# Moving the weight transfers of the third and fourth expert: two into the last quarter of attention, the rest between the late gathers

## The chip, the cores and the metric

The kernel runs on 1 core of one Trainium2 chip. The metric is the device time of one execution in microseconds (us), the median of three runs. The engines are TensorE (PE; its weight loads are listed as PEld), VectorE (DVE), ScalarE (ACT), GpSimd (POOL) and SyncE (SP). POOL and SP also issue DMA transfers.

## The reference

Causal attention over 4 batches, 8 heads, 768 positions and head size 64. Three heads attend to everything before them, five only to 4 sink positions and a window of 64. The result, as 3072 tokens of 512 features, goes through a mixture of experts: each token is sent to the one of 8 experts that its domain number names.

```python
def _attn_ref(q, k, v, is_retrieval, n_sink, window):
    scores = scale * np.matmul(q, k.transpose(0, 1, 3, 2))
    ...
    mask = np.where(retr[0, :, 0, 0, None, None], full_mask, stream_mask)
    scores = np.where(mask[None, :, :, :], scores, -1000000000.0)
    ...
    return np.matmul(a, v).astype(np.float32)

def _moe_ref(x, domain_id, w1, w2):
    for e in range(E):
        mask = domain_id == e
        h = np.maximum(x[mask] @ w1[e], 0.0)
        out[mask] = h @ w2[e]
```

## The kernel before, in words

**Attention.** Two heads of one batch make a pair; there are 16 pairs, n = 0 to 15. In iteration n the kernel first calls `hooks(n)` (line 751), then computes the scores of pair n and, between them on PE, the transposes of pair n+1 (`t_items`) and the product with v of pair n-1 (`av_items`). `hooks(n)` asks SP for the loads of pair n+4, POOL for the casts to fp16 of q and k of pair n+2 and of v of pair n+1, and then for the weight transfers listed in `ws` (line 764). When a batch is done, `store_x` writes its tokens to the internal DRAM tensor `x_tok` through SP. `hooks(14)` also gathers the first four token groups of experts 0 and 1.

**Experts.** Experts are taken in pairs `pr`. Seven gathers of 128 rows (`load_xe(pr, g)`, indirect DMAs issued by POOL) bring the tokens of a pair from `x_tok`; group 6 holds the last 64 rows of each of the two experts. `x_transpose(pr, g)` turns them on PE, `layer1(e, c0, c1)` multiplies by w1 and applies the relu, `layer2(e)` multiplies by w2, copies each 128x512 block from PSUM into an `oute` buffer on DVE (four such buffers) and scatters it to the output by an indirect DMA issued by POOL (`finish_group`). `layer2_half(pr)` does group 6 of both experts.

**Weights.** `load_w(e, which)` brings w1 or w2 of expert e (numbered from 0), 2 MB of fp32 in DRAM, as 1 MB of fp16. POOL issues it, because it converts. There are four w1 buffers and four w2 buffers, so w1 of expert 4 waits until expert 0 has used its own.

**What sets the order.** The schedule is manual: on each engine, instructions run in the order in which the program writes them. POOL runs the casts, the weight transfers, the gathers and the scatters in that one order, and all of its transfers go into the one DMA queue q0; the loads and stores of SP go into q1. After attention the order for POOL is: three gathers of pair 0 (lines 799 and 800), seven gathers of pair 1 (line 803), then w2 of expert 1, w1 and w2 of expert 2, w1 and w2 of expert 3 (lines 805 to 808), w1 of experts 4 and 5 (line 813), seven gathers of pair 2 (line 824), w1 of expert 6 (line 827), and only then the three scatters of expert 0.

Of the kernel before, what the change touches and what calls it, by code (L numbers as in the profile page):

```python
# [21 lines left out]
def kernel(  # L22
# [117 lines left out]
    def load_qk(n):  # L140
        b, pi = divmod(n, 4)
        hA, hB = PAIRS[pi]
        for nm, src in (("q", q), ("k", k)):
            t = qkpool.tile([P, 2, NSO, D], FP32, tag=nm, name=f"{nm}32_{n}")
            nc.sync.dma_start(
                out=t[:].rearrange("p h t d -> p h (t d)"),
                in_=hsel(src, b, hA, hB).rearrange("h (p t) d -> p h (t d)", p=P),
            )
            q32_t[nm, n] = t

    def cast_qk(n, engs=None):
        for x, nm in enumerate("qk"):
            t = tpool.tile([P, NSO, 2, D], FP16, tag=f"{nm}16", name=f"{nm}_{n}")
            eng = engs[x] if engs else nc.gpsimd
            eng.tensor_copy(  # L155
                out=t[:].rearrange("p t h d -> p h t d"), in_=q32_t[nm, n][:]
            )
            qk_t[nm, n] = t

    def load_v(b, pi):  # L160
        hA, hB = PAIRS[pi]
        t = vpool.tile([P, 2, NSO, D], FP32, tag="v32", name=f"v32_{b}_{pi}")
        for hh, h in enumerate((hA, hB)):
            nc.sync.dma_start(
                out=t[:, hh], in_=v[b, h].rearrange("(c p) d -> p c d", p=P)
            )
        v_t[b, pi] = t

    def cast_v(b, pi):
        if pi == 0:  # L170
            ve_t[b] = vepool.tile([P, NSO, H, D + 1], FP16, tag="ve", name=f"ve_{b}")
            vs_t[b] = vepool.tile([36, H, D + 1], FP16, tag="vs", name=f"vs_{b}")
            nc.gpsimd.memset(ve_t[b][:, :, :, D : D + 1], 1.0)
        hA, hB = PAIRS[pi]
        for hh, h in enumerate((hA, hB)):
            nc.gpsimd.tensor_copy(out=ve_t[b][:, :, h, 0:D], in_=v_t[b, pi][:, hh])  # L176

    def load_w(e, which):
        if which == 1:
            t = wpool.tile([P, 2, 2, F], FP16, tag="w1", name=f"w1_{e}")  # L180
            nc.gpsimd.dma_start(
                out=t[:].rearrange("p c r f -> p c (r f)"),
                in_=moe_w1[e].rearrange("(c p r) f -> p c (r f)", p=P, r=2),
            )
        else:
            t = wpool.tile([P, 2, 4, DM], FP16, tag="w2", name=f"w2_{e}")
            nc.gpsimd.dma_start(
                out=t[:].rearrange("p c r d -> p c (r d)"),
                in_=moe_w2[e].rearrange("(c p r) d -> p c (r d)", p=P, r=4),
            )  # L190
        w_t[e, which] = t
# [75 lines left out]
    def t_items(n):  # L267

        items = []
        for nm, store in (("q", qT), ("k", kT)):  # L270
            cell = {}

            def tr(t, nm=nm, store=store, cell=cell):
                if t == 0:
                    cell["ps"] = ps_t.tile([P, NSO, P], FP16, tag="tp", name=f"tp{nm}_{n}")
                nc.tensor.transpose(  # L276
                    out=cell["ps"][:, t, :], in_=qk_t[nm, n][:, t].rearrange("p h d -> p (h d)"), identity=id_sb
                )
                if t == NSO - 1:
                    d = tpool.tile([P, P, NSO], FP16, tag=f"{nm}T", name=f"{nm}T_{n}")  # L280
                    nc.vector.tensor_copy(  # L281
                        out=d[:], in_=cell["ps"][:].rearrange("d t p -> d p t")
                    )
                    store[n] = d[:].rearrange("d p t -> d (p t)")
                    ra, rb = (retr[h] for h in PAIRS[n % 4])
                    if nm == "k" and not ra and not rb:
                        ks = ks_t[n % 2]
                        nc.vector.tensor_copy(out=ks[0:64, 0:4], in_=store[n][0:64, 0:4])
                        nc.vector.tensor_copy(
                            out=ks[64:128, 32:36], in_=store[n][64:128, 0:4]  # L290
                        )

            for t in range(NSO):
                items.append((60, lambda t=t, tr=tr: tr(t)))
        return items
# [114 lines left out]
    def store_x(b):  # L410
        nc.sync.dma_start(
            out=x_d[1 + b * S : 1 + (b + 1) * S, :].rearrange("(t p) d -> p t d", p=P), in_=xb[b][:]
        )
# [211 lines left out]
    NG = PAIRSLOTS // P  # L625

    def load_xe(pr, g, nb=B):
        if pr not in xe_t:
            xe_t[pr] = vepool.tile([P, NG, DM], FP16, tag="ve", name=f"xe_{pr}")
        s = pr * NG + g  # L630
        nc.gpsimd.indirect_dma_start(  # L631
            out=xe_t[pr][:, g, :],
            out_offset=None,
            in_=x_d[0 : 1 + nb * S, :],
            in_offset=bass.IndirectOffsetOnAxis(ap=map_i[:, s : s + 1], axis=0),
            bounds_check=nb * S,
            oob_is_err=False,
        )
# [23 lines left out]
    def layer1(e, c0, c1):  # L662
        if e not in hT_t:
            hT_t[e] = epool.tile([P, 8, CAP], FP16, tag="eT", name=f"hT_{e}")
        for f2 in range(4):
            ps = ps_s.tile([P, 1024], FP32, tag="sp", name=f"h1_{e}_{f2}_{c0}")
            pv = ps[:].rearrange("p (a c) -> p a c", a=2)
            for a in range(2):
                fc, fr = divmod(2 * f2 + a, 4)
                for c in range(4):  # L670
                    nc.tensor.matmul(  # L671
                        out=pv[:, a, c0:c1],
                        lhsT=w_t[e, 1][:, c // 2, c % 2, fc * 512 + fr : (fc + 1) * 512 : 4],
                        rhs=xT_t[e][:, c, c0:c1],
                        start=(c == 0),
                        stop=(c == 3),
                    )
            nc.scalar.activation(  # L678
                out=hT_t[e][:, 2 * f2 : 2 * f2 + 2, c0:c1], in_=pv[:, :, c0:c1], func=AF.Relu
            )  # L680
# [30 lines left out]
    def layer2_half(pr):  # L711
        ps = ps_a.tile([P, 512], FP32, tag="av", name=f"o2h_{pr}")
        for f in range(8):
            for i in range(2):
                e = 2 * pr + i
                nc.tensor.matmul(
                    out=ps[i * HALF : (i + 1) * HALF, :],
                    lhsT=hT_t[e][:, f, MAIN:CAP],
                    rhs=w_t[e, 2][:, f // 4, f % 4, :],
                    start=(f == 0),  # L720
                    stop=(f == 7),
                    skip_group_check=True,
                )
        finish_group(pr, 6, ps)
# [23 lines left out]
    def vs_copy(b):  # L748
        nc.vector.tensor_copy(out=vs_t[b][32:36], in_=ve_t[b][0:4, 0])

    def hooks(n):
        b, pi = divmod(n, 4)
        if n + 4 < NPAIR:
            load_qk(n + 4)
            load_v((n + 4) // 4, (n + 4) % 4)
        if n + 2 < NPAIR:
            cast_qk(n + 2)
        if n + 1 < NPAIR:
            cast_v((n + 1) // 4, (n + 1) % 4)
        if pi == 3:  # L760
            vs_copy(b)
        if n >= 5 and n % 4 == 1:
            store_x(n // 4 - 1)
        ws = {4: (0, 1), 8: (1, 1), 12: (0, 2)}
        if n in ws:
            load_w(*ws[n])
        if n == 14:
            for g in (0, 1, 3, 4):
                load_xe(0, g, 3)

    for _, fn in t_items(0):
        fn()
# [27 lines left out]
        load_xe(0, g)  # L800
    for e in range(N_EARLY):
        layer1(e, 0, EARLY)
    for g in range(NG):
        load_xe(1, g)
    load_w(1, 2)
    for e in (2, 3):
        load_w(e, 1)
        load_w(e, 2)
    for g in (2, 6, 5):
        x_transpose(0, g)  # L810
    for e in range(N_EARLY):
        layer1(e, EARLY, CAP)
        load_w(e + 4, 1)
    for e in range(E):
        pr, i = divmod(e, 2)
        nxt = e + 2
        if i == 1:
            layer2_half(pr)
        if nxt < E:
            if i == 0:  # L820
                for g in range(7):
                    x_transpose(pr + 1, g)
                if pr + 2 < E // 2:
                    [load_xe(pr + 2, g) for g in range(NG)]
            layer1(nxt, 0, CAP)
            if nxt + 4 < E:
                load_w(nxt + 4, 1)
        layer2(e)
        if e + 4 < E:
            load_w(e + 4, 2)  # L830
# [96 lines left out]
```

## Time and profile before

| | us |
|---|---|
| median of 3 runs | 257.03 |
| lowest and highest of them | 255.66, 266.19 |
| the profiled execution, device time | 254.73 |
| its span, first to last instruction | 253.0 |
| PE busy in it | 202.8 (80%) |
| POOL busy | 110.2 (44%) |
| DVE busy | 105.5 (42%) |
| ACT busy | 92.6 (37%) |

All positions in the text are microseconds from the start of that span. Busy shares are averages over stages with different limits; a busy PE is not PE at its peak.

### The profile page before, as it was taken

To read this page: it belongs to the slowest core of one execution; us is meant where nothing else is said; L and a number is where in the kernel's file an instruction comes from. 1 tells how busy PE (TensorE), PEld (TensorE's weight loads), DVE (VectorE), ACT (ScalarE), POOL (GpSimd) and SP (SyncE) were. 2 spreads that over 40 slices of the span, in tenths; PEclk is the share of its full clock that TensorE was granted. 3 is DMA by queue.
4 is the path that set the end of the run, shared out by engine and by line. 5 is a ranking of instruction groups with operands and counts; after the bars stand their busy time and mean duration, and the time that the engine had idled before them with its cause. 6 is when DMAs were issued, how large, how long until landed. Compare 5 with 4: busy or idle time off the path is not lost. (4 is left out here: it accounts for less than half of the span.)

```text
span 253.0 us, 4605 instructions
## 1 busy us (share of the span) xinstructions
PE 202.8 (80%) x1871; PEld 120.8 (48%) x1871; DVE 105.5 (42%) x242; ACT 92.6 (37%) x109; POOL 110.2 (44%) x143
## 2 busy tenths in 40 slices
PE   1589899988999999869604999507899979999960
PEld 0246556655666666869401545203545445454420
DVE  1259999997578576501400031004222150403330
ACT  2277547744875876253200504100222305050000
POOL 0557564562455523067932122364757140414550
PEclk9999959997999999997955899956999999999995
DMA  6999999999999842233599999899995856212421
GB/s 218 299 311 305 285 294 254 329 322 244 293 325 226 153 142 72 78 109 97 109 214 216 211 216 216 209 227 237 271 265 174 167 155 135 92 36 84 156 86 37
DMA packets 45467, 49.77 MB, mean 197 GB/s; under 512 B 27263, under 2 KB 38784, under 8 KB 45442
## 3 DMA queue, kind: packets, MB, share of 16 engines
q0 software_dynamic: 7936, 26.75, 45.9%
q1 hardware_dynamic: 36928, 22.02, 31.6%
q10 hardware_dynamic: 578, 0.66, 0.9%
q8 instruction: 16, 0.26, 0.4%
q14 instruction: 9, 0.07, 0.1%
HBM read 56.76 MB, written 10.49 MB: 266 GB/s over the span
## 5 line engine op out<-in xcount | busy, mean ns | idle before, releaser
L332 ACT ACTIVATE eT<-sp 128x1024 f16<-128x1024 f32 (+2 forms) x68 | 60.5, 916 | 35.4 <-PE sp L311 34.8
L678 ACT ACTIVATE hT<-h 128x896 f16<-128x896 f32 (+2 forms) x40 | 30.7, 768 | 96.1 <-PE h L671 96.1
L671 PE MATMUL h<-xT,w 128*128 128x448 f16 (+2 forms) x320 | 54.0, 331 | 11.6 <-DMA w<-in_moe_w_dram 10.8
L684 DVE COPY oute<-o 128x512 f32<-128x512 f32 x24 | 16.6, 692 | 88.5 <-PE o L702 70.1
L702 PE MATMUL o<-w,hT 128*128 128x512 f16 x192 | 44.4, 389 | 10.0 <-DVE oute L684 10.0
L631 POOL DMA_INDIRECT xe<-x_tok,map_i x28 | 28.4, 1013 | 47.9 <-DMA w<-in_moe_w_dram 23.8
L671 PEld LDWEIGHTS <-w 128*128 128x128 f16 x320 | 35.2, 117 | 29.3 <-DMA w<-in_moe_w_dram 11.0
L686 POOL DMA_INDIRECT out_dram<-oute,out_i x28 | 27.9, 997 | 42.4 <-DVE oute L684 37.1
L702 PEld LDWEIGHTS <-hT 128*128 128x128 f16 x192 | 19.0, 99 | 33.6 <-issue 12.4
L386 PE MATMUL av<-ve,eT 128*128 128x65 f16 (+3 forms) x532 | 31.8, 198 | 3.2 <-DVE xb L399 3.2
L386 PEld LDWEIGHTS <-eT 128*128 128x128 f16 (+3 forms) x572 | 25.9, 101 | 13.8 <-issue 4.1
L311 PE MATMUL sp<-qT,kT 64*128 64x192 f16 (+6 forms) x244 | 26.7, 282 | 1.8 <-DVE kT L281 1.2
L311 PE MATMUL sp<-c16s 128*128 128x128 f16 (+1 forms) x132 | 25.9, 279 | 0.4 <-ACT eT L332 0.3
L155 POOL CAST q<-q 128x768 f16<-128x768 f32 x15 | 12.9, 862 | 30.6 <-PE tpq L276 14.5
L281 DVE COPY qT<-tpq 128x768 f16<-128x768 f16 x16 | 15.3, 954 | 7.6 <-PE tpq L276 7.5
L399 DVE TENSOR_TENSOR xb<-av,rcp 128x384 f16<-128x384 f32 x32 | 17.8, 557 | 1.1
L155 POOL CAST k<-k 128x768 f16<-128x768 f32 x16 | 13.5, 842 | 9.9 <-DMA k<-in_k_dram 8.0
L311 PEld LDWEIGHTS <-kT 64*128 64x128 f16 x244 | 9.7, 95 | 16.1 <-issue 7.0
L281 DVE COPY kT<-tpk 128x768 f16<-128x768 f16 x16 | 15.2, 948 | 3.6 <-PE tpk L276 3.6
L176 POOL CAST ve<-v 128x384 f16<-128x384 f32 x32 | 16.0, 528 | 0.7 <-DMA v<-in_v_dram 0.7
L654 DVE COPY xT<-xtp 128x512 f16<-128x512 f16 x24 | 9.1, 418 | 15.2 <-PE xtp L647 14.2
L647 PE MATMUL xtp<-c16s,xe 128*128 128x128 f16 x112 | 10.3, 226 | 6.2 <-DVE xT L654 3.1
(71 smaller groups left out, 123.6 us busy)
## 6 DMA issues: line engine op xcount, KB each, us to landing
w<-in_moe_w_dram POOLq DMA_DIRECT2D x16, 1024.0 KB, 11.3
q<-in_q_dram SPq DMA_DIRECT2D x16, 384.0 KB, 6.0
k<-in_k_dram SPq DMA_DIRECT2D x16, 384.0 KB, 6.0
v<-in_v_dram SPq DMA_DIRECT2D x32, 192.0 KB, 5.7
x_tok<-xb SPq DMA_DIRECT2D x4, 768.0 KB, 6.0
xe<-x_tok,map_i POOLq DMA_INDIRECT x28, 4.8
out_dram<-oute,out_i POOLq DMA_INDIRECT x28, 2.8
c16s<-c ACTq DMA_DIRECT2D x1, 336.5 KB, 4.6
```

What stands on the lines that cost most here:

```text
L155: eng.tensor_copy(out=t[:].rearrange("p t h d -> p h t d"), in_=q32_t[nm, n][:])
L281: nc.vector.tensor_copy(out=d[:], in_=cell["ps"][:].rearrange("d t p -> d p t"))
L311: nc.tensor.matmul(out=sp[:, c : c + w], lhsT=lhsT, rhs=rhs, start=bank not in begun, stop=True, skip_group_check=True,)
L332: nc.scalar.activation(out=eT[n][:, r, c0:c1], in_=sp[:, c0:c1], func=AF.Exp, scale=scale)
L386: nc.tensor.matmul(out=ps[m0:m1, it, :], lhsT=eT[n][kk, r, c : c + w], rhs=rhs, start=(x == 0), stop=(x == len(mms) - 1), skip_group_check ...
L399: nc.vector.tensor_tensor(out=xb[b][:, :, h * D : (h + 1) * D], in0=ps[:, :, 0:D], in1=rcp[:].unsqueeze(2).to_broadcast([P, NSO, D]), op=A ...
L631: nc.gpsimd.indirect_dma_start(out=xe_t[pr][:, g, :], out_offset=None, in_=x_d[0 : 1 + nb * S, :], in_offset=bass.IndirectOffsetOnAxis(ap= ...
L671: nc.tensor.matmul(out=pv[:, a, c0:c1], lhsT=w_t[e, 1][:, c // 2, c % 2, fc * 512 + fr : (fc + 1) * 512 : 4], rhs=xT_t[e][:, c, c0:c1], st ...
L678: nc.scalar.activation(out=hT_t[e][:, 2 * f2 : 2 * f2 + 2, c0:c1], in_=pv[:, :, c0:c1], func=AF.Relu)
L684: nc.vector.tensor_copy(out=o[:], in_=ps[:])
L686: inst = nc.gpsimd.indirect_dma_start(out=out, out_offset=bass.IndirectOffsetOnAxis(ap=out_i[:, s : s + 1], axis=0), in_=o[:], in_offset=None,
L702: nc.tensor.matmul(out=ps[:], lhsT=hT_t[e][:, f, g * P : (g + 1) * P], rhs=w_t[e, 2][:, f // 4, f % 4, :], start=(f == 0), stop=(f == 7),)
```

## The change

Six weight transfers are issued at other places in POOL's order; nothing is added or removed. w2 of expert 0 goes from `hooks(12)` to `hooks(11)`; w1 of expert 2 takes its place in `hooks(12)`; w2 of expert 1 follows the four gathers in `hooks(14)`. After attention, w1 of expert 3 is issued ahead of the gathers of pair 1, w2 of expert 2 between the fourth and the fifth of these gathers, and w2 of expert 3 after w1 of expert 4.

```diff
-        ws = {4: (0, 1), 8: (1, 1), 12: (0, 2)}
+        ws = {4: (0, 1), 8: (1, 1), 11: (0, 2), 12: (2, 1)}
         if n in ws:
             load_w(*ws[n])
         if n == 14:
             for g in (0, 1, 3, 4):
                 load_xe(0, g, 3)
+            load_w(1, 2)
...
     for e in range(N_EARLY):
         layer1(e, 0, EARLY)
-    for g in range(NG):
+    load_w(3, 1)
+    for g in range(4):
         load_xe(1, g)
-    load_w(1, 2)
-    for e in (2, 3):
-        load_w(e, 1)
-        load_w(e, 2)
+    load_w(2, 2)
+    for g in range(4, NG):
+        load_xe(1, g)
     for g in (2, 6, 5):
         x_transpose(0, g)
     for e in range(N_EARLY):
         layer1(e, EARLY, CAP)
         load_w(e + 4, 1)
+        if e == 0:
+            load_w(3, 2)
```

## Rows read from the trace of the kernel before

**Rows 1.** PE in order of time, second half: start, length, operation, [idle before <-releaser]

```profile
121.59 0.61 PE L647 MATMUL xtp<-c16s,xe 128*128 128x128 f16 x8
...
136.36 8.62 PE L671 MATMUL h<-xT,w 128*128 128x448 f16 x32 [10.78 <-DMA w<-in_moe_w_dram]
...
158.02 3.62 PE L702 MATMUL o<-w,hT 128*128 128x512 f16 x16
171.67 3.57 PE L702 MATMUL o<-w,hT 128*128 128x512 f16 x8 [10.04 <-DVE oute L684]
175.04 0.77 PE L647 MATMUL xtp<-c16s,xe 128*128 128x128 f16 x8
...
178.93 6.24 PE L671 MATMUL h<-xT,w 128*128 128x448 f16 x32 [0.39 <-DVE xT L657]
```

**Rows 2.** The waits by engine: who waited for what, us, times, longest

```profile
DVE oute L684 <- DMA out_dram<-oute,out_i: 18.5, 2, 18.2
```

**Rows 3.** POOL in order of time, from the end of attention

```profile
109.08 1.00 POOL L631 DMA_INDIRECT xe<-x_tok,map_i  x1 [11.32 <-SPq L833]
...
121.82 0.78 POOL L187 DMA_DIRECT2D w<-in_moe_w_dram  x1
...
125.36 1.53 POOL L181 DMA_DIRECT2D w<-in_moe_w_dram  x2
127.19 1.08 POOL L631 DMA_INDIRECT xe<-x_tok,map_i  x1 [0.30 <-issue]
132.26 1.04 POOL L631 DMA_INDIRECT xe<-x_tok,map_i  x1 [3.99 <-DMA w<-in_moe_w_dram]
...
161.31 0.75 POOL L181 DMA_DIRECT2D w<-in_moe_w_dram  x1 [4.16 <-DMA w<-in_moe_w_dram]
```

**Rows 4.** Issues with KB, us to landing: at 126.05, 127.19, 156.16, 161.31, 205.53

```profile
w<-in_moe_w_dram POOLq DMA_DIRECT2D x1, 1024.0 KB, 34.7
xe<-x_tok,map_i POOLq DMA_INDIRECT x1, 34.0
xe<-x_tok,map_i POOLq DMA_INDIRECT x1, 7.2
w<-in_moe_w_dram POOLq DMA_DIRECT2D x1, 1024.0 KB, 8.8
w<-in_moe_w_dram POOLq DMA_DIRECT2D x1, 1024.0 KB, 7.9
```

**Rows 5.** Stretches: length, engines' busy us (instructions), PEclk, DMA share, GB/s

```profile
112.00:122.00 10.00, 8.48 (x84) 7.78 (x85) 1.34 (x4) 3.74 (x9) 7.87 (x9) 0.83 0.36 105
126.00:136.00 10.00, 0.00 (x0) 0.00 (x0) 0.10 (x1) 0.00 (x0) 3.01 (x4) 0.58 1.05 209
144.80:161.60 16.80, 16.80 (x89) 8.30 (x88) 2.77 (x4) 4.58 (x5) 3.29 (x4) 1.00 1.05 235
```

**Rows 6.** POOL in order of time, last quarter of attention

```profile
77.68 0.83 POOL L155 CAST q<-q 128x768 f16<-128x768 f32 x1 [1.89 <-PE tpq L276]
...
80.15 0.71 POOL L187 DMA_DIRECT2D w<-in_moe_w_dram  x1
...
92.70 1.09 POOL L631 DMA_INDIRECT xe<-x_tok,map_i  x1 [7.00 <-DVE xb L399]
```

**Rows 7.** DMA queues by packets, MB, share: 58 to 64, then 77 to 82

```profile
q0 software_dynamic: 227, 0.93, 78.3%
q1 hardware_dynamic: 492, 0.54, 29.2%
...
q1 hardware_dynamic: 2049, 1.05, 80.7%
```

**Rows 8.** Issue view: SP's last v load, issued at 76.16

```profile
v<-in_v_dram SPq DMA_DIRECT2D x1, 192.0 KB, 5.7
```

**Rows 9.** PE in order of time, end of attention

```profile
92.76 0.51 PE L276 MATMUL tpq<-c16s,q 128*128 128x128 f16 x6
...
101.82 0.72 PE L647 MATMUL xtp<-c16s,xe 128*128 128x128 f16 x8 [0.65 <-DVE xT L654]
```

## The prediction

> **What bounds the kernel now.** I read the timeline of PE first, because PE is the busiest engine (80% of the span) and the question is where it stands still. After attention two gaps carry nearly all of it [rows 1]: 10.78 us before the first layer of expert 2 at 136.36, ended by a weight transfer, and 10.04 us in the middle of layer 2 of expert 1 at 171.67, ended by a copy into an output buffer on DVE. From 175.04 to the end PE runs with small gaps only.
>
> I then ask what each gap waits for at its source. The first is a transfer by its name: w1 of expert 2, second of seven weight transfers that POOL issues in a row between 121.82 and 126.05 [rows 3]. The second is POOL's order: DVE waited 18.2 us for a scatter to read its buffer out [rows 2], and the scatters stand in POOL's queue behind seven gathers of pair 2 and w1 of expert 6. The gather at 127.19 goes out at once, the next at 132.26 only when a weight has landed, and w1 of expert 6 at 161.31 likewise [rows 3]. Counting places from the first of the seven weights, the gather at 132.26 is the ninth: each issue waits here for the one eight places ahead to land. So POOL is held until the last of the seven, issued at 126.05 and 34.7 us under way, lands at 160.8 [rows 4].
>
> Two prices come out of the same rows. Seven gathers and one weight released one by one between 132.26 and 161.31 make 29.05 / 6 = 4.8 to 4.9 us for each weight in a chain. That the queue is served in order shows in the gather issued at 127.19, which lands 34.0 us later at 161.2, just behind the last weight; the last of that gather group lands at 156.16 + 7.2 = 163.4 [rows 4], so a gather queued in this way costs (163.4 - 161.2) / 6 = 0.37 us. A weight alone takes 7.9 to 8.8 us [rows 4]. The stretch from 126 to 136 shows the DMA engines full (share 1.05) with PE at zero [rows 5]: in that stage the kernel is bound by q0.
>
> **Step 1: two weights in late attention.** w2 of expert 0 is now issued when the casts of `hooks(11)` are done, at 77.68 - 1.89 = 75.8, and w1 of expert 2 in the old slot at 80.15 [rows 6]. For POOL this is free: an issue takes 0.7 to 0.8 us and the slot at 75.8 has 1.89 us of idle time. What it meets is SP's loads. From 77 to 82 q1 still moves 1.05 MB, and the last v load lands at 76.16 + 5.7 = 81.9 [rows 7, 8]. While a weight ran beside SP's loads, from 58 to 64, q1 got 0.54 MB in 6 us, 90 GB/s [rows 7]. At that rate 1.05 MB take 11.7 us and land at 88.7, 7 us later than now. Cover: pair 15 is transposed on PE at 92.76 [rows 9], 4 us later, and its q and k, which SP loads ahead of v, can be cast before the last v load lands. So nothing reaches PE. The store of batch 2 shares its time with the second weight; I let the first gather slip 1.9 us from 92.70 [rows 6]. PE takes the last two of these four groups at 101.82 [rows 9], after idling for a copy and not for a gather: price 0, with an upper bound of 2 us, the whole slip, if that cover is gone.
>
> The Trainium skill ("DMA: Bandwidth & Descriptors", sections "Queues, rings and completion order" and "Issuing engines are not separate DMA queues") speaks against this step: all issuing engines share the same 16 DMA engines, and these take turns between queues packet by packet. The trace shows the sharing but not even turns: 227 packets of q0 beside 492 of q1 [rows 7]. With strict turns q1 would move 227 packets of its mean 1.1 KB in those 6 us, an estimate of 42 GB/s in place of 90, and the last load would come some 2 us after 88.7, when the two weights are through; by either the sum stays as it is, but the cover of 4 us is halved.
>
> **Step 2: w2 of expert 1 in `hooks(14)`.** It follows four gathers, at about 99.5, and lands near 108. PE needs it only after layer 2 of expert 0. The store of batch 3 overlaps its end; three gathers of pair 0 wait for that store now at 109.08 [rows 3]. I add 0.5 us there, bounds 0 and 1.5, and PE waits for these gathers in both kernels, so it counts in full.
>
> **Step 3: the late chain.** It now has five weights ahead of the gathers of pair 2, not seven, and starts at 113.4 (109.6 plus three gathers; ten of them took 109.08 to 121.82 [rows 3], 1.27 each), not at 121.82. w1 of expert 3 lands 7.9 to 8.8 us later at 121.3 to 122.2; the four gathers behind it by 122.8 to 123.7, about when PE, which takes them at 121.59 now [rows 1], is ready at 122.1. w2 of expert 2, issued at about 119.3, follows in the queue: 122.8 + 4.9 = 127.7. The last three gathers of pair 1 land behind it by 128.8. This is a wait which the change adds: what PE could have at 125.6 (136.36 - 10.78) it gets 3 us later. With transposes and a copy, about 0.9 us, layer 1 of expert 2 starts at 129.7, where it started at 136.36: 6.7 us gained. If the gathers were not held by the second weight the start would be 126; if both weights took 8.8 us, 134.5 (113.4 + 17.6 + 2.6 for seven gathers + 0.9).
>
> The clock: before, the granted clock is 0.58 over the idle stretch [rows 5] and this layer took 8.62 us, against 6.24 at 178.93 [rows 1], so 2.4 were lost. After, PE idles about 4 us ahead of it. Much shorter gaps left 0.83 over 112 to 122 [rows 5], a half-speed stretch of 3.4 us of 10; I take 8.2 us for the layer, bounds 6.24 and 8.62. It ends at 137.9.
>
> **Step 4: the second gap.** From there PE has 16.8 us of work without a gap (144.80 to 161.60 [rows 5]) plus one block of eight matmuls: 3.57 us now, half of 3.62 = 1.8 at full clock [rows 1]. If nothing holds it, the transposes of pair 2 start at 137.9 + 16.8 + 1.8 = 156.5, against 175.04. What holds it is the chain: after 128.8, w1 of expert 4, w2 of expert 3 and w1 of expert 5 at 4.9 each end at 143.5. That landing releases w1 of expert 6 at 143.8, 17.5 us earlier than 161.31; it lands 8.8 later at 152.6. Now it lands at 161.31 + 8.8 = 170.1 [rows 4], the scatters behind it, and PE goes on 1.6 us later at 171.67 [rows 1]; so PE could go on at 154.2, and it gets to that block at 137.9 + 16.8 = 154.7: just hidden, with half a microsecond to spare. Price 0, bounds 0 and 5; w1 of experts 4 and 5 wait for used buffers, free by 122.5, so that adds none.
>
> **Step 5: the rest.** After 175.04 the same work follows in the same order with every weight of it issued at least as early; gain and loss 0.
>
> **Sum.** 175.04 - 156.5 = 18.5 us of the span of 253.0. The profiled execution took 254.73 with what lies around its span, so 236.2 by that. The median of the runs is 257.03 and the lowest 255.66; I carry the 0.9 us of the lowest: **237 us**.
>
> **The rivals.**
>
> *The second gap stays in part (chance 0.14).* The weight chain slips by up to 8 us because single weights between gathers run nearer 7.9 than 4.9. The margin in step 4 is half a microsecond, so all of it returns as a wait for an output buffer: 242 to 246. For it: a lone weight costs 7.9. Against: the queue is never empty after 119, and a chain costs 4.9.
>
> *The loads of attention starve (0.05).* Two weights hold SP's loads and the store of batch 2. Place: the transposes of pair 15 and of pair 0's first gathers. It decides once the loads land after 92.76. The price is bounded by the DMA time of the two weights, 2 x 4.9 = 9.8 us: 247. Against: the cover of 4 us. (By the rule of the Trainium skill cited in step 1 this is the rival that comes closer.)
>
> *Slower than before (0.03).* Weights and gathers mixed in one queue lose the chain pace altogether: each of the five costs x in place of 4.9. The last lands at 113.4 + 5x + 2.6; it is as late as today's 160.8 at x = 9.0, and from there the second gap grows past its present size. At x = 10.4 it lands at 168.0, 7.2 us worse than now: 263. Against: seven in a row ran at 4.9, and lone ones at 7.9 to 8.8.
>
> *It does not do what it says (0.04).* If the first gap had another cause behind the transfer, both gaps would only move: within 2% of 257. The landing of that weight and the start of PE agree in rows 1, so little is left for it.
>
> *Better than forecast (0.08).* The gathers slip past w2 of expert 2 and the clock holds: layer 1 of expert 2 at 126. The scatters then bind: PE goes on at 154.2, or up to 2 us earlier if w1 of expert 6 lands in 7.9 us and each weight of the chain in 4.8. That caps the gain at some 21 us: 234 to 235; the low end leaves 2 us for the spread of the runs.
>
> **How the numbers follow.** The forecast itself, 235 to 241, has 0.66. The range takes in the better case and the second gap's return: 232 to 246. Faster by over 2% (about what a measurement of this kernel can tell from no change) takes all but the last rival pair: 0.93, same 0.04, slower 0.03.
>
> **What would show it.** Right: PE's gap at 136 gone, one of 3 to 5 us near 124 to 129 that ends on gathers of pair 1, no wait of layer 2 on `oute` over 2 us, POOL's first scatter near 144, transposes of pair 2 near 156.5. Wrong in step 1: gaps of PE between 92 and 103. Wrong in step 3: chain spacing other than 4.9, or the gathers landing before the weight ahead of them. Wrong in step 4: the gap of layer 2 still there.

## The result, and the profile after

The changed kernel takes 242.26 us (median of four runs, 240.77 to 246.35); the kernel before took 258.37 beside it (four runs, 255.66 to 266.19). The ratio is 0.943, with a 95% interval of 0.930 to 0.956. The forecast was 237, its range 232 to 246. The profiled execution of the changed kernel took 241.41 us with a span of 239.6; against 253.0 that is 13.4 us gained where 18.5 were expected. Some profiled executions of the experiments have a long stretch of attention at half clock; only lengths behind that stretch are compared, and ratios leave disturbed runs out.

Cut the span at four marks of PE's timeline (the transposes of pair 0, the first matmuls of layer 1 of expert 0, layer 1 of expert 2, the transposes of pair 2) and compare piece by piece:

| stage, us | before | after |
|---|---|---|
| start to transposes of pair 0 | 100.54 | 100.42 |
| to layer 1 of expert 0 | 3.67 | 5.79 |
| to layer 1 of expert 2 (first gap) | 32.15 | 27.86 |
| to transposes of pair 2 (second gap) | 38.68 | 27.68 |
| to the end | 77.91 | 77.88 |

PE in order of time in the changed kernel (start, length, operation, and in brackets the idle time before it and what ended it), the rows that answer to [rows 1, 9]:

```profile
92.64 0.51 PE L276 MATMUL tpq<-c16s,q 128*128 128x128 f16 x6
...
100.42 0.62 PE L647 MATMUL xtp<-c16s,xe 128*128 128x128 f16 x8
103.27 0.71 PE L647 MATMUL xtp<-c16s,xe 128*128 128x128 f16 x8 [2.23 <-DVE xT L654]
106.22 9.68 PE L671 MATMUL h<-xT,w 128*128 128x256 f16 x64
...
124.69 0.67 PE L647 MATMUL xtp<-c16s,xe 128*128 128x128 f16 x8
130.85 1.04 PE L647 MATMUL xtp<-c16s,xe 128*128 128x128 f16 x8 [4.01 <-DMA xe<-x_tok,map_i]
133.08 0.61 PE L647 MATMUL xtp<-c16s,xe 128*128 128x128 f16 x4 [1.20 <-DMA xe<-x_tok,map_i]
134.07 8.46 PE L671 MATMUL h<-xT,w 128*128 128x448 f16 x32 [0.39 <-DVE xT L657]
...
155.58 3.62 PE L702 MATMUL o<-w,hT 128*128 128x512 f16 x16
160.03 1.89 PE L702 MATMUL o<-w,hT 128*128 128x512 f16 x8 [0.84 <-DVE oute L684]
161.76 0.61 PE L647 MATMUL xtp<-c16s,xe 128*128 128x128 f16 x8
```

Both gaps of the kernel before are gone. The one that ended on a weight (10.78 us) has become two waits of 4.01 and 1.20 us that end on gathers of pair 1, and the one of 10.04 us on an output buffer is down to 0.84. But layer 1 of expert 2 starts only 2.3 us earlier than before, and PE is later than before where layer 1 of expert 0 begins. POOL in order of time shows why, in the rows that answer to [rows 3, 6]:

```profile
75.62 0.72 POOL L187 DMA_DIRECT2D w<-in_moe_w_dram  x1
...
80.03 0.72 POOL L181 DMA_DIRECT2D w<-in_moe_w_dram  x1
...
92.51 0.51 POOL L176 CAST ve<-v 128x384 f16<-128x384 f32 x1 [0.65 <-DMA v<-in_v_dram]
...
96.27 1.09 POOL L631 DMA_INDIRECT xe<-x_tok,map_i  x1 [2.53 <-DVE xb L399]
...
101.32 0.78 POOL L187 DMA_DIRECT2D w<-in_moe_w_dram  x1
112.42 1.05 POOL L631 DMA_INDIRECT xe<-x_tok,map_i  x1 [10.32 <-SPq L836]
116.09 0.78 POOL L181 DMA_DIRECT2D w<-in_moe_w_dram  x1
122.13 0.79 POOL L187 DMA_DIRECT2D w<-in_moe_w_dram  x1
...
139.51 1.00 POOL L631 DMA_INDIRECT xe<-x_tok,map_i  x1 [3.73 <-DMA w<-in_moe_w_dram]
144.32 1.00 POOL L631 DMA_INDIRECT xe<-x_tok,map_i  x1 [3.81 <-DMA w<-in_moe_w_dram]
149.46 0.75 POOL L181 DMA_DIRECT2D w<-in_moe_w_dram  x1 [4.14 <-DMA w<-in_moe_w_dram]
150.51 1.03 POOL L686 DMA_INDIRECT out_dram<-oute,out_i  x1 [0.30 <-DVE oute L684]
```

The first gather has moved from 92.70 to 96.27, the gather behind the store of batch 3 from 109.08 to 112.42. The cast of v at 92.51 waits for a load, which no cast of late attention did before. The two DMA queues from 82 to 90 (packets, MB, time of their packets as a share) are the row that answers to [rows 7]:

```profile
q0 software_dynamic: 372, 1.45, 89.0%
q1 hardware_dynamic: 411, 0.37, 17.1%
```

SP's queue (q1) got 0.37 MB in 8 us, 46 GB/s, beside the weights in q0. Its last v load, issued at 77.90, answers to [rows 8], in the view of issues:

```profile
v<-in_v_dram SPq DMA_DIRECT2D x1, 192.0 KB, 15.3
```

It landed at 93.2, not at 88.7 as forecast, and not at 81.9 as before. Those four and a half microseconds use up the cover that step 1 counted on. But PE did not meet the late loads themselves: the transposes of pair 15 came at 92.64 (92.76 before) and those of pair 0 at 100.42. What met them is the store of batch 2, which SP issued at 87.52 while its own loads were still under way.

### The profile page after: what moved, and what is told of

The parts are those of the page before. It is cut to its first block, busy times and chain, and to the rows that moved or that the text cites. A ratio compares the mean times of both kernels' runs of the same rounds, so it can differ in the third digit from the quotient of the medians.

```text
span 239.6 us, 4605 instructions
## 1 busy us (share of the span) xinstructions
PE 201.2 (84%) x1871; PEld 119.6 (50%) x1871; DVE 106.0 (44%) x242; ACT 92.4 (39%) x109; POOL 111.3 (46%) x143
## 5 line engine op out<-in xcount | busy, mean ns | idle before, releaser
L671 PE MATMUL h<-xT,w 128*128 128x448 f16 (+2 forms) x320 | 55.4, 335 | 1.8 <-DVE xT L657 1.2
L702 PE MATMUL o<-w,hT 128*128 128x512 f16 x192 | 42.8, 379 | 0.8 <-DVE oute L684 0.8
L631 POOL DMA_INDIRECT xe<-x_tok,map_i x28 | 28.5, 1019 | 30.1 <-DMA w<-in_moe_w_dram 10.5
L311 PE MATMUL sp<-qT,kT 64*128 64x192 f16 (+6 forms) x244 | 26.2, 278 | 2.4 <-DVE kT L281 1.7
L155 POOL CAST q<-q 128x768 f16<-128x768 f32 x15 | 13.0, 868 | 26.5 <-DMA q<-in_q_dram 12.3
L155 POOL CAST k<-k 128x768 f16<-128x768 f32 x16 | 14.1, 879 | 19.9 <-DMA k<-in_k_dram 13.1
```

Of the source, the lines that this page charges most:

```text
L155: eng.tensor_copy(out=t[:].rearrange("p t h d -> p h t d"), in_=q32_t[nm, n][:])
L311: nc.tensor.matmul(out=sp[:, c : c + w], lhsT=lhsT, rhs=rhs, start=bank not in begun, stop=True, skip_group_check=True,)
L631: nc.gpsimd.indirect_dma_start(out=xe_t[pr][:, g, :], out_offset=None, in_=x_d[0 : 1 + nb * S, :], in_offset=bass.IndirectOffsetOnAxis(ap= ...
L671: nc.tensor.matmul(out=pv[:, a, c0:c1], lhsT=w_t[e, 1][:, c // 2, c % 2, fc * 512 + fr : (fc + 1) * 512 : 4], rhs=xT_t[e][:, c, c0:c1], st ...
L702: nc.tensor.matmul(out=ps[:], lhsT=hT_t[e][:, f, g * P : (g + 1) * P], rhs=w_t[e, 2][:, f // 4, f % 4, :], start=(f == 0), stop=(f == 7),)
```

## The experiments

My theory: the moves do what the prediction says, and the missing 5.1 us are a collision, SP's loads and stores sharing the DMA engines with the weights of late attention, together with the gathers of pair 1 held by w2 of expert 2. The rival: the gain comes from one part of the change alone, or from freeing output buffers, and the order of the weights matters little. The edits are shown against the changed kernel, except the one that is made in the kernel before; `...` stands for lines left out. In what follows, "store to gather" is the time from SP's issue of the store of a batch to POOL's first gather that reads it.

**The attention part alone.** After attention, the order of before without the two weights that are already there:

```diff
-    load_w(3, 1)
-    for g in range(4):
+    for g in range(NG):
         load_xe(1, g)
     load_w(2, 2)
-    for g in range(4, NG):
-        load_xe(1, g)
+    load_w(3, 1)
+    load_w(3, 2)
...
-        if e == 0:
-            load_w(3, 2)
```

> Only the attention part of the change: w2 of expert 0, w1 of expert 2 and w2 of expert 1 go early as in the changed kernel; after attention all seven gathers of pair 1 go first, then w2 of expert 2, w1 and w2 of expert 3, w1 of experts 4 and 5. Theory (the first gap goes with the early weights, the second follows the end of the late chain): the first gap is gone, layer 1 of expert 2 starts near 129.5; the chain starts near 125, ends near 155, the second gap is 12 to 13 us; 248 to 250 us. Rival (the second gap goes because weights were taken out of the chain, whatever the place of the rest): second gap below 3 us, 240 to 243 us.

Median 255.72 us (251.16 to 256.44) beside 260.73; the profile showed a second gap of 6.41 us and stalls of PE in layer 1. It ran once more:

> The kernel of e1 once more, beside the two others, because TensorE stood still for 5 us in layer 1 in that profile for no cause that the profile names. If that belonged to the execution: from layer 1 of expert 0 to that of expert 2 23 to 25 us, from there to the transposes of pair 2 35 to 38 us with a second gap of 9 to 12 us, 248 to 252 us. If it belonged to the program: 28 and 33 us again.

The second time it took 249.62 (247.51 to 251.34) beside 258.84, a ratio of 0.960, interval 0.946 to 0.974. PE in order of time there shows the second gap still standing:

```profile
165.06 3.57 PE L702 MATMUL o<-w,hT 128*128 128x512 f16 x8 [8.35 <-DVE oute L684]
```

From layer 1 of expert 0 to that of expert 2 it took 27.33 us, as the changed kernel, and the next stage 34.62, against 27.68. So this part alone buys what the change buys at the first gap, and only a part of the second. If the stalls had belonged to the first execution, 23 to 25 us and a second gap of 9 to 12 were expected; but they came again, 3.7 us in all (2.98 and 2.04 the first time). The changed kernel loses about as much there by waiting for gathers, so that the two lengths agree is luck.

**The late part alone.** Attention as before; w1 of expert 2 ahead of the gathers of pair 1, w2 of expert 1 between the fourth and the fifth:

```diff
-        ws = {4: (0, 1), 8: (1, 1), 11: (0, 2), 12: (2, 1)}
+        ws = {4: (0, 1), 8: (1, 1), 12: (0, 2)}
...
-            load_w(1, 2)
...
-    load_w(3, 1)
+    load_w(2, 1)
     for g in range(4):
         load_xe(1, g)
-    load_w(2, 2)
+    load_w(1, 2)
     for g in range(4, NG):
         load_xe(1, g)
+    load_w(2, 2)
+    load_w(3, 1)
+    load_w(3, 2)
...
-        if e == 0:
-            load_w(3, 2)
```

> Only the interleaving of the late part: attention as before; w1 of expert 2 ahead of the gathers of pair 1, w2 of expert 1 between the fourth and fifth of them, then w2 of expert 2, w1 and w2 of expert 3 and the rest as before. Theory (the late chain starts 9 us earlier but keeps seven weights): layer 1 of expert 2 near 129.7, the chain ends near 153, second gap near 9 us, 246 to 249 us; no slip in attention (first gather near 92.7, store of batch 3 near 105.1). Rival (the slip in attention seen in the changed kernel is not due to the early weights): the same slip of 3 us here.

252.76 (251.79 to 258.73) beside 260.73: ratio 0.975, interval 0.963 to 0.987; 246 to 249 had been expected. The first gather went at 92.57, without the slip, so the slip belongs to the early weights. From layer 1 of expert 0 to that of expert 2 it took 26.46 us, even less than the changed kernel, but the second gap stayed nearly whole:

```profile
167.91 3.57 PE L702 MATMUL o<-w,hT 128*128 128x512 f16 x8 [9.58 <-DVE oute L684]
```

0.960 x 0.975 = 0.936, against 0.943 for both together: the parts add, so the gain does not come from one of them. With seven weights in q0 after attention instead of five the second gap stands, behind the gathers as before or among them as here.

**The weights of attention one iteration later.**

```diff
-        ws = {4: (0, 1), 8: (1, 1), 11: (0, 2), 12: (2, 1)}
+        ws = {4: (0, 1), 8: (1, 1), 12: (0, 2), 13: (2, 1)}
```

> The changed kernel with its first two moved weights one hook later: w2 of expert 0 in iteration 12 (its old place), w1 of expert 2 in iteration 13. Theory (two weights side by side with the last loads of q, k and v starve them, which costs 3.3 us at the gathers of pair 0): the last v load lands near 82 to 84 in place of 93, the first gather goes near 94 in place of 96.3, the first gather after attention near 109.5 to 110.5 in place of 112.4, 2 to 3 us less than the changed kernel: 239 to 240 us. Rival (w2 of expert 1 beside the store of batch 3 makes the slip): that gather stays near 112, 242 us.

245.05 (241.42 to 250.02), ratio 0.939, interval 0.924 to 0.953: no better than the change; the 239 to 240 us that were expected did not come. In the profiled execution a half-clock stretch (60.9 to 74.6) made PE some 6 us late. There the last v load landed in good time, at 85.6, but w1 of expert 2, issued at 90.62, met the store of batch 2, issued at 93.5:

```profile
103.96 1.09 POOL L631 DMA_INDIRECT xe<-x_tok,map_i  x1 [11.65 <-DVE vs L749]
```

Store to gather was 10.43 us here and 5.06 before. In these two profiles the second weight meets SP's loads in one place and its store in the other; moving it by one iteration only chose which.

**Eight output buffers in the kernel before**, with all weights where they were:

```diff
-        o = opool.tile([P, DM], FP32, tag="oute", name=f"oute_{pr}_{g}")
+        pool, tag = ((opool, "oute"), (vpool, "v32"))[g % 2]
+        o = pool.tile([P, DM], FP32, tag=tag, name=f"oute_{pr}_{g}")
```

> The kernel before with eight output buffers in place of four (every second one lies in the buffers of the v loads, which are free by then); nothing moved. Theory (the second gap is a wait for an output buffer, and the scatter that frees it is queued behind the weight chain): the 10 us gap of layer 2 of expert 1 goes, the transposes of pair 2 start when their gathers land, 163.5 in place of 175.0, 242 to 245 us. Rival (the gap is the bandwidth of the queue, and buffers only move it to the next transfer): another wait of 5 us or more for a gather or a weight after 163, 249 us or more.

245.30 (244.47 to 251.52) beside 260.73: ratio 0.949, interval 0.939 to 0.959. The block of layer 2 that waited at 171.67 [rows 1] is no longer parted from the rest:

```profile
164.47 5.34 PE L703 MATMUL o<-w,hT 128*128 128x512 f16 x24
169.65 0.61 PE L647 MATMUL xtp<-c16s,xe 128*128 128x128 f16 x8
```

The transposes of pair 2 start 62.4 us behind those of pair 0 (107.26 in this profile), where the kernel before took 74.5 and 63.0 were expected. The scatters still stand in POOL's queue behind w1 of expert 6, issued at 168.68, and PE does not wait for them. So the second gap was a wait for a buffer, behind it POOL's order, as step 4 read it; four more buffers are worth nearly as much as the whole change.

**The changed kernel once more**, beside the next two.

> The changed kernel itself, a second profile beside the others of this call. If the lengths of its stages belong to the program, they come back: from the store of batch 2 to the first gather 8 to 9 us, from the start of layer 1 of expert 0 to that of expert 2 27 to 28.5 us, from there to the transposes of pair 2 26.5 to 28.5 us, from there to the end 77.5 to 79.5 us; near 242 us. If they come from the clock of one execution, they differ by 2 us or more.

240.86 (239.96 to 243.03) beside 257.31: 0.9425, interval 0.933 to 0.952. The time came back, and the stage to layer 1 of expert 2 (28.09 us), but not all lengths did: store to gather was 6.89 us, where 8 to 9 were expected, and the stage to the transposes of pair 2 29.15, where 26.5 to 28.5 were, with a second gap of

```profile
160.17 3.37 PE L702 MATMUL o<-w,hT 128*128 128x512 f16 x8 [1.97 <-DVE oute L684]
```

And in this profile PE did not pay for the slip of the first gather. It was 2 us late already at the transposes of pair 9 (62.00, 59.85 in the first profile), ahead of the two weights, came to the transposes of pair 0 at 102.43, and then idled 0.66 us, as before the change, not 2.23. The gather behind the store of batch 3 went at 112.49 all the same, and layer 1 of expert 2 started at 134.18, both as in the first profile.

**w2 of expert 2 behind all gathers of pair 1.**

```diff
     load_w(3, 1)
-    for g in range(4):
+    for g in range(NG):
         load_xe(1, g)
     load_w(2, 2)
-    for g in range(4, NG):
-        load_xe(1, g)
```

> The changed kernel with w2 of expert 2 issued behind all seven gathers of pair 1, not between the fourth and the fifth. Theory (the wait of 5 us for the last gathers is the weight ahead of them in the queue, and the chain then holds the output buffers): from layer 1 of expert 0 to that of expert 2 22.5 to 24.5 us in place of 27.9; the second gap comes back at 4 to 7 us, so the whole stays within 2 us of the changed kernel. Rival (the chain ends earlier too, as nothing else is queued): second gap below 2 us, 4 us faster than the changed kernel.

244.77 (243.74 to 246.21): ratio 0.960, interval 0.950 to 0.970. PE in order of time:

```profile
130.43 7.93 PE L671 MATMUL h<-xT,w 128*128 128x448 f16 x32 [0.39 <-DVE xT L657]
...
161.61 3.46 PE L702 MATMUL o<-w,hT 128*128 128x512 f16 x8 [6.60 <-DVE oute L684]
164.91 0.61 PE L647 MATMUL xtp<-c16s,xe 128*128 128x128 f16 x8
```

Of the waits on the gathers (3.41 and 1.10 us in the run above) 0.49 and 1.39 are left: the stage to layer 1 of expert 2 took 22.48 us where the run above took 28.09. The next stage took 34.48 where that one took 29.15, with a second gap of 6.60. Nearly all of what is gained where the weight no longer stands between the gathers is given back one stage later: of the two waits, the buffer's is the bound. The two stages add to 56.96 and 57.24, so the 4 us by which this kernel is slower in the median, outside the 2 us expected, do not come from there; that stays open.

Its attention showed something else. The two weights were issued at 79.47 and 83.88, later than in the changed kernel, because PE had run 13.7 us of attention at half clock; the loads of SP were in by 82.7, and store to gather was 5.05. The queues of this kernel from 84 to 88 hold the weight alone, nothing of SP:

```profile
q0 software_dynamic: 210, 0.79, 103.2%
```

Over all six runs with two weights in these two places, by the time of the first weight's issue:

| kernel | first weight issued | store issued | last v load in | store to gather, us |
|---|---|---|---|---|
| attention part again | 74.86 | 86.76 | 92.62 | 8.99 |
| changed | 75.62 | 87.52 | 93.17 | 8.75 |
| changed again | 77.62 | 89.52 | 93.00 | 6.89 |
| behind, eight buffers | 78.00 | 89.90 | 95.17 | 8.14 |
| behind | 79.47 | 91.37 | 82.66 | 5.05 |
| attention part | 81.60 | 93.50 | 85.62 | 5.20 |

Every run with one weight there has 4.94 to 5.09, the kernel before 5.06. So it is the collision with SP's last loads that holds the store and the gathers, as the theory has it. The issue time of the weight does not order the rows; what does is the time for which loads are still under way after the store's issue: 3.48, 5.27, 5.65 and 5.86 us make 6.89, 8.14, 8.75 and 8.99, and where the loads are in, there is no slip. In the two rows without it a half-clock stretch of attention had made PE, and with it weights and store, late beside the loads; no edit made that difference.

**A third weight in late attention**, to double the suspected cost:

```diff
-        ws = {4: (0, 1), 8: (1, 1), 11: (0, 2), 12: (2, 1)}
+        ws = {4: (0, 1), 8: (1, 1), 11: (0, 2), 12: (2, 1), 13: (1, 2)}
...
-            load_w(1, 2)
```

> The changed kernel with w2 of expert 1 issued in iteration 13, ahead of the first gathers, not behind them: three weights beside the last loads and the store of batch 2. Theory (early weights hold the loads, the store and the gathers by the DMA time they take): the first gather some 5 us later than in the changed kernel, 13 us or more after the store of batch 2 is issued; PE waits 3 to 6 us more in the transposes of pair 0; from the store of batch 3 to the next gather 4 us in place of 5.3; 2 to 4 us slower than the changed kernel. Rival (PE hides it): no change.

242.72 (240.79 to 245.94): ratio 0.950, interval 0.935 to 0.965, 2 us over the changed kernel of the same chip by the medians; the intervals overlap. The first gather went at 96.16, not 5 us later as expected. POOL in order of time shows what stood in the way:

```profile
91.38 0.83 POOL L155 CAST k<-k 128x768 f16<-128x768 f32 x1 [3.69 <-DMA k<-in_k_dram]
```

POOL sat in the queue for a cast whose load was late, so it issued the third weight only at 93.06, when the last v load was in (92.77). It did not test the price that it was made to double; what it shows is that the collision limits itself, since POOL, which issues the weights, also waits for the loads that they hold up.

**One weight in late attention, the other behind the gathers of batch 2**, w2 of expert 1 behind the gathers of pair 1, four output buffers:

```diff
-        ws = {4: (0, 1), 8: (1, 1), 11: (0, 2), 12: (2, 1)}
+        ws = {4: (0, 1), 8: (1, 1), 12: (0, 2)}
...
-            load_w(1, 2)
+            load_w(2, 1)
...
     for g in range(4, NG):
         load_xe(1, g)
+    load_w(1, 2)
```

> The changed kernel with one weight less in late attention: w2 of expert 0 back in iteration 12, w1 of expert 2 behind the first gathers in iteration 14, w2 of expert 1 behind the last gathers of pair 1; four output buffers. Theory (the early weights cost the slip before layer 1 of expert 0, but each weight taken out of the late chain is worth 4.9 us of the second gap): first gather 5 us after the store of batch 2, near 91 to 93, the slip of some 3 us gone; the chain one weight longer, second gap 3 to 6 us; within 2 us of the changed kernel. Rival (the slip has nothing to do with the early weights): first gather 7 us or more after the store, 3 us slower than the changed kernel.

250.27 (249.27 to 258.03) beside 258.84: ratio 0.965, interval 0.957 to 0.974, 2.2 points worse than the change, where the two were expected within 2 us. Store to gather was 5.09, as expected, but one weight more stood in the late chain:

```profile
173.18 3.57 PE L702 MATMUL o<-w,hT 128*128 128x512 f16 x8 [5.63 <-DVE oute L684]
```

A weight taken out of the late chain is worth more than the slip that it causes in attention. Undoing the collision this way costs more than it saves, as long as output buffers bind.

**The two cures together.** Eight output buffers, one weight early, and the late order rearranged so that the gathers of pair 1 come soon:

```diff
-        o = opool.tile([P, DM], FP32, tag="oute", name=f"oute_{pr}_{g}")
+        pool, tag = ((opool, "oute"), (vpool, "v32"))[g % 2]
+        o = pool.tile([P, DM], FP32, tag=tag, name=f"oute_{pr}_{g}")
...
-        ws = {4: (0, 1), 8: (1, 1), 11: (0, 2), 12: (2, 1)}
+        ws = {4: (0, 1), 8: (1, 1), 12: (0, 2)}
...
-            load_w(1, 2)
+            load_w(2, 1)
...
-    load_w(3, 1)
-    for g in range(4):
+    load_w(1, 2)
+    for g in range(NG):
         load_xe(1, g)
+    load_w(3, 1)
     load_w(2, 2)
-    for g in range(4, NG):
-        load_xe(1, g)
...
-        load_w(e + 4, 1)
         if e == 0:
-            load_w(3, 2)
+            load_w(4, 1)
...
                     [load_xe(pr + 2, g) for g in range(NG)]
+                if e == 0:
+                    load_w(3, 2)
+                    load_w(5, 1)
```

> All findings together: eight output buffers; w2 of expert 0 in iteration 12 as before the change, w1 of expert 2 behind the first gathers in iteration 14; after attention w2 of expert 1 ahead of the seven gathers of pair 1, then w1 of expert 3, w2 of expert 2, w1 of expert 4, the gathers of pair 2, and only then w2 of expert 3 and w1 of expert 5. Theory: no starving of the loads (first gather 5 us after the store of batch 2), from layer 1 of expert 0 to that of expert 2 22.5 to 24.5 us, from there to the transposes of pair 2 24.5 to 26 us with no wait for an output buffer: 230 to 235 us. Rival (the weights, 16 of 4.9 us each, bind in the end): new waits of PE for w1 of expert 3 or 4, 238 us or more.

231.85 (231.10 to 236.99, six runs) beside 257.31: ratio 0.908, interval 0.899 to 0.916, the best of all. PE in order of time:

```profile
98.90 0.62 PE L647 MATMUL xtp<-c16s,xe 128*128 128x128 f16 x8
...
102.57 7.25 PE L671 MATMUL h<-xT,w 128*128 128x256 f16 x64
...
125.21 7.88 PE L671 MATMUL h<-xT,w 128*128 128x448 f16 x32 [0.39 <-DVE xT L657]
...
146.12 5.34 PE L703 MATMUL o<-w,hT 128*128 128x512 f16 x24
151.30 0.61 PE L647 MATMUL xtp<-c16s,xe 128*128 128x128 f16 x8
```

No wait for a weight, none for a buffer; all loads of attention had landed by 83.5 and store to gather was 5.04. Transposes of pair 2 start 10.5 us earlier than in the changed kernel. Of these, 1.5 are attention itself, which has no half-clock stretch between 39.8 and 125.2 here; 2.1 lie in the transposes of pair 0, and 5.2 and 1.6 in the two stages behind.

**The change with w2 of expert 2 behind the gathers and eight buffers** leaves out the cure of attention:

> The kernel of e6 (w2 of expert 2 behind the seven gathers of pair 1) with the eight output buffers of e4. Theory (two waits share one chain, so that taking away the first only fed the second): from layer 1 of expert 0 to that of expert 2 22.5 to 24.5 us as in e6, from there to the transposes of pair 2 25 to 27 us in place of 34.5; 6 to 8 us faster than the changed kernel, 233 to 236 us. Rival (the gathers of pair 2 behind the chain bind just as much as the buffers): 29 us or more for that stage, 238 us or more.

Its edit is that of "w2 of expert 2 behind all gathers of pair 1" together with that of "Eight output buffers". 237.83 (237.04 to 239.40) beside 258.84: ratio 0.915, interval 0.907 to 0.923; 233 to 236 us had been expected. The two stages took 25.88 and 24.47 us, where w2 behind the gathers with four buffers had 22.48 and 34.48: the second gap is gone, so it was the buffers that took back what moving this weight gained. The change as it is, with eight buffers, was not run. Two losses are left in it, and how they share what it lacks to the best kernel, whose late order differs too, is not shown: store to gather was 8.14, and layer 1 ran with stalls such as this one in PE's timeline:

```profile
130.02 1.44 PE L671 MATMUL h<-xT,w 128*128 128x192 f16 x8 [2.06 <-ACT hT L678]
```

## Why the prediction was right, and where it was off

The sign, the mechanism of the two gaps and the range held; the size fell short by 5.1 us in the span (234.5 forecast, 239.6 measured). **The term that was mis-sized first is the collision in late attention**: step 1's "At that rate 1.05 MB take 11.7 us and land at 88.7" and its "price 0", measured as 2.0 us; then come step 2's half microsecond (1.3) and step 3's three gathers at 0.37 us each.

**Step 1.** SP's rate of 90 GB/s beside a weight was read from 58 to 64 [rows 7], and this reading was wrong: for the first of these six microseconds the weight had hardly begun to move. From 58 to 59 q1 moved 305 of its 492 packets, beside 13 of q0. From 59 to 64 the same trace of before has

```profile
q0 software_dynamic: 214, 0.88, 87.3%
q1 hardware_dynamic: 187, 0.27, 17.1%
```

These are even turns, and 54 GB/s. In the changed kernel it was 46, with 411 packets of q1 beside 372 of q0. The Trainium skill ("DMA: Bandwidth & Descriptors", section "Queues, rings and completion order") says that the DMA engines alternate between queues packet by packet. The trace agrees with the rate that the prediction estimated from that, 42 GB/s; the landing that it put beside it, some 2 us after 88.7, was still 2.5 us too early.

The last load landed at 93.2, behind the 92.76 that step 1 gave as the end of its cover, and yet pair 15 was transposed on time. The loss came by the store of batch 2, which step 1 let share its time with the second weight alone: it stood beside the loads, and the first gather slipped 3.6 us instead of 1.9. PE's gap ahead of the third group of pair 0 was 2.23 us, where [rows 9] had 0.65, and layer 1 of expert 0 began 2.0 us later than before: step 1's upper bound, not its price. That this layer ran in part at half clock (granted 0.5 from 104.5 to 111.3; 9.68 us for the 64 matmuls, 7.25 in the second profile) cost no more: in both profiles PE then waits for gathers of pair 0, and layer 1 of expert 2 starts at the same time.

**Step 2.** Forecast 109.6 for the gather behind the store of batch 3, measured 112.42. Of the 2.8 us too many, 2.0 come from the store, issued at 107.14 and not 105.13 because PE was late, so they are step 1's price; 0.8 from step 2 itself: store to gather took 5.28 us, against 3.94 before; that is 1.3 more instead of 0.5, inside its bounds of 0 and 1.5. Of the 1.3, 0.8 lie in the store itself (4.5 us from issue to landing, 3.7 before), which is the overlap that step 2 named.

**Step 3.** The chain began where the sum puts it behind that gather (116.09 - 112.42 = 3.67, forecast 3.8), and the wait it announced stands where it said, on gathers of pair 1. Layer 1 of expert 2 started at 134.07 and not 129.7: 2.8 of the 4.4 are inherited from step 2, and 1.55 lie in the two weights and seven gathers, which took longer than the 7.9 + 1.5 + 4.9 + 1.1 us taken. Most of that is in the last three gathers: in the second profile w2 of expert 2 landed at 130.7, and PE had the last of them at 133.19, 2.5 us later and not 1.1. The layer took 8.46, against 8.2 taken and bounds of 6.24 and 8.62.

**Step 4.** The chain's pace was right: 139.51, 144.32, 149.46 are 4.8 and 5.1 us apart, for 4.9. w1 of expert 6 was released at 149.46 (forecast 143.8), 5.7 us late, and PE was ready for its block 4.5 us late, so the margin of half a microsecond turned into a wait of 0.84 (1.97 in the second profile). That the wait of 10.04 was a buffer's was shown by the eight buffers, and that the weights in q0 set when it ends by the runs in which the gap came back: 9.58 with seven weights after attention, 5.63 with six, 8.35 and 6.41 with five that all start behind the gathers of pair 1, and 6.60 with four of the five behind them.

**Step 5.** 77.88 against 77.91: right.

Added up by the starts of the rows: 4.4 + 0.1 (the layer, 8.3 us to the start of the next row) + 0.8 (the second gap) = 5.3 late at the transposes of pair 2, of which 0.1 came back behind them.

**The rivals.** "The loads of attention starve" got 0.05 and was the true direction: its condition, loads landing after 92.76, came true, at about a third of its price of 10 (2.8 us at the gather behind the store of batch 3). It got so little because the cover was judged from the rate that was misread. "The second gap stays in part" named 242 to 246, and the measured 242.26 lies in it, but by luck: the gap came back as 0.84 us, and its reason, a late chain whose pace falls from 4.9 to 7.9, did not come. "Slower" and "does not do what it says" fall with the chain's pace. Of the two theories behind the experiments, the collision is borne out by the table of store and loads, with two amendments: what w2 of expert 2 costs between the gathers is no part of the missing 5.1 us, since the buffers take it back; and the 2.0 us that PE paid are shown in one of the two profiles of the changed kernel, since in the other PE was late for another reason and the slip was hidden. The rival falls where it says one part, and holds in part where it says buffers: these alone do nearly as much as the change.

## What to carry to other kernels

Take the rate that a queue keeps beside another from the packet counts of a stretch in which both are full all the time: one microsecond too many made 90 GB/s of 54 here. Count the landing of the last load against the first instruction that needs it, store and gather included. Before transfers are reordered to empty a queue sooner, ask what the waiting engine really lacks: here four more output buffers alone gave 5%. A wait taken away one stage early is given back at the next bound, so two bounds in a row have to be lifted together: one edit here took 5.6 us out of one stage and put 5.3 into the next, and only with more buffers did both come out short.

## What the runs showed of the hardware that was not expected

- PE's granted clock in attention differs between executions, and this moved the collision. These are the stretch from 56 to 76 in two of the runs above (length, busy times with instruction counts, granted clock, DMA share, GB/s), first w2 behind the gathers, then the changed kernel again:

```profile
56.00:76.00 20.00, 18.19 (x179) 10.69 (x180) 10.96 (x28) 10.62 (x12) 5.79 (x10) 0.66 1.10 280
```

```profile
56.00:76.00 20.00, 17.77 (x248) 11.45 (x244) 13.99 (x34) 12.37 (x14) 7.74 (x14) 0.91 1.10 278
```

  PE was busy all the while in both, 18.19 and 17.77 of 20 us, with 0.66 and 0.91 of its clock. What makes the one fall to 1.2 GHz for 13.7 us was not found.
- In both runs with eight buffers other than the best, and in both runs of the attention part, PE stood still inside layer 1 of pair 0 for up to 2.98 us at a time, some 3 to 5 us in all, ended by ACT's relu or by nothing that the profile names; before the change there was none, and the changed kernel has one of 0.61. The cause was not found.
- Store to gather for batch 3 was 4.45 us in the best kernel, against 3.94 before, though the store itself took 3.7 us to land in both. The half microsecond lies between its landing and the gather: 0.77 us instead of 0.26. It is 0.77 in every run that has issued at least one weight more by then than the kernel before, and 0.26 in the other two, as before; it is also the other part of the 1.3 in step 2. The cause was not found.
